# Twelve unread small products and a re-planned first part in a decayed linear attention with two feed-forward layers

## The chip, the cores and the metric

One core of a Trainium2 chip runs the whole program. The metric is device time in microseconds from one launch; lower is better. Several executions are timed, and one of them is profiled.

## The reference

A recurrent attention over 4 batches, 8 heads, 768 steps and 48 features, then two feed-forward layers over the 3072 tokens of width 384:

```python
for t in range(S):
    cur = einsum('bhd,bhe->bhde', u[None] * kt, vt)
    y[:, :, t] = einsum('bhd,bhde->bhe', rt, state + cur)
    state = wt[:, :, :, None] * state + einsum('bhd,bhe->bhde', kt, vt)
...
h = maximum(maximum(x @ w1, x @ w2), x @ w3)          # 384 -> 768
x = h @ w_out                                         # 768 -> 384
silu = g * (1.0 / (1.0 + exp(-g)))                    # g = x @ w_gate, 384 -> 1536
out = silu * (x @ w_val) @ w_out
```

## The kernel before

**Attention.** The 768 steps are six chunks of 128 (c = 0 to 5), and a chunk has four units (a pair of heads each, in the order 3, 0, 1, 2), so 24 units n = 0 to 23. Unit 4 is the first of chunk 1. For each unit SyncE loads the decays, k and r (`load_a`, tile inpA, two DMAs, two buffers), and v (`load_v`). VectorE then runs two scans over the decays (`suffix` L366, `prefix` L379), makes the scaled k and r (`khats` L369 and L371, tile kh; `rps` L382, tile rp), and for units 0 to 7 the product rk (L426), which TensorE sums (`rk_sum` L432, tile pa) and ScalarE spreads over a diagonal (`diag` L447, tile A). TensorE transposes kh (`transposes` L469, tile kp), ScalarE copies it out (`keep`), TensorE makes the state's increment (`outer` L536, tile kv) and the scores (`scores` L455, tile sc), which VectorE writes into A under a mask (`causal` L460). The output y is built in two parts (`first_y`, and `second_y` with L495 and L508). Between them ScalarE reads two columns (`peek`). The second part needs the state decayed to the middle of the chunk: `add_state` (L549), `decay` (L393). ScalarE copies y out rounded (`upper` L557), TensorE subtracts that copy (`take_upper` L566), and the rest is kept too (`lower`).

**Feed-forward.** Every wide product is three TensorE products of 128x512 (high times high, high times low, low times high; `mm3`, L590 to L592). A piece `up(c, f, m)` is nine of them, with weight group f. The weights arrive as 64-bit floats (`wload`, two buffers). VectorE turns them to 32 bits in three steps (`bits`, L131 to L133), ScalarE rounds the high part (`whigh` L629), VectorE subtracts for the low part (`wlow` L634, tile lo). Chunk 0's pieces wait for these. `up_out` takes the maximum over m = 0, 1, 2 on VectorE (L664). `down` makes the first layer's output, with plain 32-bit products in chunk 0 (L681). Behind chunk 5's first layer only the second layer runs.

**The order.** Nothing of this is scheduled by hand. Each step is added to a `Plan` with its engine, a cost in us, its dependencies, a due time, and the accumulator buffers (`slot`) it takes of a pool of four (`psM`). `Plan.order` simulates the engines with these costs and emits the steps in the order of their simulated starts; each engine then executes its own in that order. Among steps that can start about as early it takes the one with the lowest due time plus 15 times the start; `STAY` takes 2.0 off for a step of the same `kind` as the engine's last. The attention's products on TensorE have kind 1, all else kind 0. Every unit has a due time of its own (`due`).

**Guards.** ScalarE checks the decays' range (`watch`, two passes over 128x512), in place for units 8 to 23, and for units 0 to 7 from a second load late in the program (`watch_load`).

Of the kernel before, what the change touches and what calls it, by code (L numbers as in the profile page):

```python
# [9 lines left out]
F32 = mybir.dt.float32  # L10
# [4 lines left out]
AF = mybir.ActivationFunctionType  # L15
# [7 lines left out]
NT = 512  # L23
D = 48
G = 4
# [12 lines left out]
class Plan:  # L38
# [4 lines left out]
    SLOTS = 4  # L43
    STAY = 2.0

    def __init__(self):
        self.items = []

    def add(self, eng, cost, fn, deps=(), due=None, lat=0.1, slot=0, after=0.0, slack=0.0, kind=0):
        t = dict(kind=kind, eng=eng, cost=cost, fn=fn, deps=[d for d in deps if d is not None], due=due, lat=lat,  # L50
                 slot=slot, after=after, slack=slack, readers=[], id=len(self.items), start=None, end=None)
        self.items.append(t)
        return t
# [6 lines left out]
    def order(self):  # L60
# [18 lines left out]
        for t in reversed(topo):  # L79
            dates = [n["due"] - n["cost"] - t["lat"] for n in t["next"]] + [t["due"] or far]  # L80
            t["due"] = min(dates)
        free, last, dma, slots, out = {}, {}, 0.0, [], []
        for t in items:
            t["todo"] = len(t["deps"])
        avail = [t for t in items if not t["todo"]]
        while avail:
# [14 lines left out]
            for t in avail:  # L101
                if t.get("at") is not None and t["at"] <= best + 0.3:
                    k = first.get(t["eng"])
                    t["key"] = t["due"] + 15 * t["at"] - self.STAY * (t["kind"] == last.get(t["eng"]))
                    if k is None or t["key"] < k["key"]:
                        first[t["eng"]] = t
# [3 lines left out]
            avail.remove(t)  # L110
            last[t["eng"]] = t["kind"]
            t["start"] = t["at0"]
# [162 lines left out]
def fused(ctx: ExitStack, tc: tile.TileContext, pk, ub, wt_all, out):  # L275
# [264 lines left out]
    def add_state(n, s):  # L540
        c, j = units[n]
        if c == 0 and s == 0:
            decay(n, 0)
            for g in range(G):
                nc.scalar.activation(
                    states[n][1][:, g, :], kvs[n][0][:, g, :], AF.Copy, scale=total[n % 2][:, 2 * g + 1:2 * g + 2]
                )
        else:
            nc.vector.tensor_tensor(states[n][1] if s == 0 else S[j], states[n][s], kvs[n][s], ALU.add)  # L549
# [98 lines left out]

    hh, hl, hws, pss = {}, {}, {}, {}

    def up(c, f, m):
# [123 lines left out]
    def on(eng, cost, fn, *args):  # L775
        return lambda deps=(), due=None, **k: p.add(eng, cost, lambda: fn(*args), deps, due, **k)
# [19 lines left out]

    chunks = list(range(8)) + [("again", i) for i in range(8)] + list(range(8, 20)) + [("late", n) for n in range(8)]
    for turn, what in enumerate(chunks):
# [53 lines left out]
    for n, (c, j) in enumerate(units):  # L852
# [3 lines left out]
        cold = 1.4 if early else 1.0  # L856
        due = 10 + 6.0 * i if early else START[c - 1] + (i + 1) * (PERIOD / 4) - (30 if c == 5 else 6 if c == 1 else 18)
        war = prev("rp", n, 2) + prev("kh", n, 2) + prev("prefix", n, 2)
# [20 lines left out]
        if c > 0:  # L879
            de = L["decay0", n] = on("DVE", 0.27, decay, n, 0)([to] + prev("state1", n, 4) + prev("y2", n, 2))  # L880
        if n >= 8:
            for k in range(2):
                L[f"watch{k}", n] = on("ACT", 0.81, watch, n, k)([la, r_])
        tr = L["tr", n] = on("PE", 0.45 * cold, transposes, n)([kh] + prev("outer", n, 1), slot=1, slack=lag, kind=1)
        kT = L["khT", n] = p.reads(on("ACT", 0.48, keep, n)([tr] + prev("outer", n, 1)), tr)
        o = L["outer", n] = on("PE", 0.55 * cold, outer, n)([kT, lv], slot=2 - c // 5, slack=lag, kind=1)
        st = L["state0", n] = on("ACT" if early else "DVE", 0.9 if early else 0.25, add_state, n, 0)([o, de or to] + (prev("y2", n, 2) if early else []))
        p.reads(st, o)
        d1 = L["decay1", n] = st if early else on("DVE", 0.27, decay, n, 1)([st, to])
        if c < NC_ - 1:  # L890
            L["state1", n] = p.reads(on("DVE", 0.25, add_state, n, 1)([o, d1], due + 2), o)
        sc_ = L["scores", n] = on("PE", 0.6 * cold, scores, n)([r_] + prev("causal", n, 1), slack=lag, kind=1)
        ca = L["causal", n] = on("DVE", 0.66, causal, n)([sc_, L["diag1", n]])
        before_y = prev("lower", n, 1)
        if n in LENT:
            before_y = [on("PE", 0.8, lend, n)(before_y + L["x", n - 3], slack=lag, kind=1)]
        y1_ = L["y1", n] = on("PE", 0.3 * cold, first_y, n)([ca, lv] + before_y, slack=lag, kind=1)
        pe = on("ACT", 0.15, peek, n)([y1_])
        y = L["y2", n] = on("PE", 0.9 * cold, second_y, n)([pe, d1], slack=lag, kind=1)

# [19 lines left out]
        if i == 3:  # L920
# [23 lines left out]
            for m, k in sorted(turns, key=lambda t: t[1]) if c == 5 else turns:  # L944
# [12 lines left out]
                L["hw", 9 * c + 6 + m] = [w2]  # L957
            L["chain"] = before


# [19 lines left out]
    for c in range(NC_):  # L980
# [58 lines left out]
        if c == 2:  # L1039
            checks = [t for k in range(8) for t in L["late", k]] + [t for i in range(8) for t in L["again", i]]  # L1040
            checks += [t for i in range(8, 20) for t in L["check", i]]
            rows = on("DVE", 0.8, check_rows)(checks, base + 30)
            mt = on("PE", 0.3, check_mat)([rows], base + 34, slot=1)
            p.reads(on("DVE", 0.2, check_end)([mt], base + 38), mt)
# [81 lines left out]
```

## Time and profile before

| | us |
|---|---|
| median of 3 runs | 865.78 |
| lowest, highest | 860.95, 868.53 |
| profiled execution, whole | 860.6 |
| its span, first to last instruction | 858.8 |
| TensorE busy in the span | 838.9 |
| VectorE busy | 426.8 |
| ScalarE busy | 342.4 |

The profile names TensorE PE, its weight loads PEld, VectorE DVE, ScalarE ACT, GpSimd POOL and SyncE SP. L590 is line 590 of the kernel. PEclk is the granted TensorE clock: 1.00 is 2.4 GHz and 0.50 is 1.2 GHz. Ends of products are modelled, so the time from one start to the next says what a product costs.

### The profile page before, as it was taken

How to read it: one execution, taken by the hardware profiler on the slowest of the kernel's cores; microseconds unless marked ns; L12 is line 12 of the kernel's file. 1: busy time of each engine (PE TensorE's matmuls, PEld its weight loads, DVE VectorE, ACT ScalarE, POOL GpSimd, SP SyncE). 2: the span in 40 equal slices, each digit the busy share in tenths (PEclk: the TensorE clock that was granted, in tenths of full speed). 3: DMA queues.
4: the chain of work that ended last, by engine and by line, in shares of the span. 5: the costliest groups of instructions: out<-in, count | busy, mean ns of one | idle time of the engine just before them, and what ended most of it. 6: DMA issues, size and time to landing. Idle time of an engine off the chain costs nothing.

```text
span 858.8 us, 15114 instructions
## 1 busy us (share of the span) xinstructions
PE 838.9 (98%) x6352; PEld 679.2 (79%) x6352; DVE 426.8 (50%) x612; ACT 342.4 (40%) x738; POOL 78.4 (9%) x104
## 2 busy tenths in 40 slices
PE   6799999999999999999999999999999999999997
PEld 5678578878788788788888888888888888888885
DVE  7899997466565666389783222222222121212121
ACT  6544565454555554454557321221232122212121
POOL 1001351211112000012000100100010010000000
PEclk9899999999999999999999999999999999999999
DMA  8766584544536542244533200010020000000001
GB/s 235 199 187 219 135 224 101 157 134 119 156 74 158 146 162 72 81 182 166 192 122 93 71 3 1 25 49 1 1 74 0 1 13 38 0 1 37 1 0 41
DMA packets 24379, 78.82 MB, mean 92 GB/s; under 512 B 3888, under 2 KB 7088, under 8 KB 20720
## 3 DMA queue, kind: packets, MB, share of 16 engines
q1 hardware_dynamic: 24304, 77.78, 30.5%
q8 instruction: 52, 0.85, 0.4%
q14 instruction: 23, 0.19, 0.1%
HBM read 66.23 MB, written 9.44 MB: 88 GB/s over the span
## 4 chain that ended last, share of the span: by engine, by line
PE 94%; DVE 2%; ACT 1%; DMA 1%; issue 1%; SPq 0%; DVEq 0%; ACTq 0%
PE ps L590 12%; PE ps L591 11%; PE ps L592 11%; PE po L590 6%; PE pv L591 6%; PE pg L591 6%; PE po L591 6%; PE pg L590 6%; PE pv L590 6%; PE po L592 6%; PE pg L592 6%; PE pv L592 6%; PE y L495 2%; PE kv L536 1%; PE sc L455 1%; PE ps L681 1%
## 5 line engine op out<-in xcount | busy, mean ns | idle before, releaser
L738 DVE TENSOR_TENSOR sil<-sil,pv 128x512 f32<-128x512 f32 x72 | 49.5, 687 | 246.3 <-PE pv L592 240.1
L590 PE MATMUL ps<-xh,hi 128*128 128x512 f32 x324 | 130.3, 402 | 0.0
L592 PE MATMUL ps<-xh,lo 128*128 128x512 f32 x324 | 126.5, 390 | 0.0
L591 PE MATMUL ps<-xl,hi 128*128 128x512 f32 x324 | 126.4, 390 | 0.0
L735 ACT ACTIVATE sil<-pg 128x512 f32<-128x512 f32 x72 | 42.9, 596 | 155.8 <-PE pg L592 155.8
L742 ACT ACTIVATE ph<-sil 128x512 fp32r<-128x512 f32 x72 | 45.4, 630 | 124.8 <-DVE sil L738 124.8
L591 PE MATMUL pg<-yl,hi 128*128 128x512 f32 x216 | 84.5, 391 | 0.0
L591 PE MATMUL pv<-yl,hi 128*128 128x512 f32 x216 | 84.5, 391 | 0.0
L591 PE MATMUL po<-pl,hi 128*128 128x512 f32 x216 | 84.5, 391 | 0.0
L590 PE MATMUL po<-ph,hi 128*128 128x512 f32 x216 | 84.4, 391 | 0.0
L590 PE MATMUL pg<-yh,hi 128*128 128x512 f32 x216 | 84.3, 390 | 0.0
L590 PE MATMUL pv<-yh,hi 128*128 128x512 f32 x216 | 84.3, 390 | 0.0
L592 PE MATMUL pg<-yh,lo 128*128 128x512 f32 x216 | 84.0, 389 | 0.0
L592 PE MATMUL po<-ph,lo 128*128 128x512 f32 x216 | 84.0, 389 | 0.0
L592 PE MATMUL pv<-yh,lo 128*128 128x512 f32 x216 | 84.0, 389 | 0.0
L747 DVE TENSOR_TENSOR pl<-sil,ph 128x512 fp32r<-128x512 f32 x72 | 49.8, 692 | 58.4 <-ACT ph L742 58.4
L590 PEld LDWEIGHTS ps<-xh,hi 128*128 128x128 f32 x324 | 60.8, 188 | 13.8
L592 PEld LDWEIGHTS ps<-xh,lo 128*128 128x128 f32 x324 | 60.8, 188 | 13.0
L591 PEld LDWEIGHTS ps<-xl,hi 128*128 128x128 f32 x324 | 60.9, 188 | 11.5
L664 DVE TENSOR_TENSOR hw<-hw,ps 128x512 f32<-128x512 f32 x60 | 40.9, 682 | 35.6 <-PE ps L592 34.0
L723 POOL TENSOR_TENSOR yl<-y,yh 128x512 fp32r<-128x512 f32 x18 | 24.2, 1348 | 353.4 <-ACT yh L719 353.3
L447 ACT ACTIVATE A<-stacked,a 128x64 f32<-128x64 f32 x192 | 49.4, 337 | 2.6 <-DVE a L419 2.4
(126 smaller groups left out, 1333.1 us busy)
## 6 DMA issues: line engine op xcount, KB each, us to landing
raw<-wt SPq DMA_DIRECT2D x28, 1152.0 KB, 5.3
inpA<-pk SPq DMA_DIRECT2D x44, 294.0 KB, 5.2
inpT<-pk SPq DMA_DIRECT2D x16, 384.0 KB, 4.6
inpV<-pk SPq DMA_DIRECT2D x24, 200.0 KB, 3.5
y1d<-y1s SPq DMA_DIRECT2D x18, 256.0 KB, 2.3
y<-y1d SPq DMA_DIRECT2D x18, 256.0 KB, 2.7
outT<-os SPq DMA_DIRECT2D x18, 256.0 KB, 2.0
wl<-pk SPq DMA_DIRECT2D x8, 272.0 KB, 2.7
```

The source lines that it names most:

```text
L447: nc.scalar.activation(A[n][:, i, :], stacked, AF.Copy, scale=sums[n][:, k:k + 1])
L455: nc.tensor.matmul(sc[n][t, a, T * g:T * g + T], khat[n][q, g, t], rp[n % 2][q, g, t], start=True, stop=True)
L495: nc.tensor.matmul(ys[n][64 * h:64 * h + rows, a, C * b + T * s:C * b + T * s + T], inpV[n][t, D * i:D * i + rows], A[n][t, i, :], start=( ...
L590: nc.tensor.matmul(ps, lh, rh, start=first, stop=False)
L591: nc.tensor.matmul(ps, lh, rl, start=False, stop=False)
L592: nc.tensor.matmul(ps, ll, rh, start=False, stop=last)
L664: nc.vector.tensor_tensor(hws[f], hws[f], pss[c, f, m], ALU.max)
L723: nc.gpsimd.tensor_tensor(yl[c, m], y1[m], yh[c, m].bitcast(F32), ALU.subtract)
L735: nc.scalar.activation(sil[f % 3], pgs[f % 3, 0], AF.Silu)
L738: nc.vector.tensor_tensor(sil[f % 3], sil[f % 3], pgs[f % 3, 1], ALU.mult)
L742: nc.scalar.activation(h_, sil[f % 3], AF.Copy)
L747: nc.vector.tensor_tensor(l_, sil[f % 3], prod[c, f][0].bitcast(F32), ALU.subtract)
```

## The change

`stir` makes eight products of the 128x128 tile `minus` with itself into an accumulator that nobody reads. Twelve of them are added to the plan at a cost of 0.6, not to start before 9, 10, ... 20 us of the plan, with due times from 36 us on. The `kind` and `STAY` rule goes. In chunk 0 the state's first half is copied by one ScalarE instruction and decayed by VectorE, in place of four scaled ScalarE copies. Units 4 to 7 are watched in place, so only four late loads remain. The due times of chunk 1's units come 12 us earlier.

```diff
-    STAY = 2.0
...
-                    t["key"] = t["due"] + 15 * t["at"] - self.STAY * (t["kind"] == last.get(t["eng"]))
-                    if k is None or t["key"] < k["key"]:
+                    if k is None or t["due"] + 15 * t["at"] < k["due"] + 15 * k["at"]:
...
-            for g in range(G):
-                nc.scalar.activation(
-                    states[n][1][:, g, :], kvs[n][0][:, g, :], AF.Copy, scale=total[n % 2][:, 2 * g + 1:2 * g + 2]
-                )
+            nc.scalar.activation(states[n][1], kvs[n][0], AF.Copy)
...
+    def stir():
+
+        ps = psM.tile([128, NT], F32, tag="mm", name="stir")
+        for k in range(8):
+            nc.tensor.matmul(ps[:, 0:128], minus, minus, start=True, stop=True)
...
-    chunks = list(range(8)) + [("again", i) for i in range(8)] + list(range(8, 20)) + [("late", n) for n in range(8)]
+    chunks = list(range(8)) + [("again", i) for i in range(8)] + list(range(8, 20)) + [("late", n) for n in range(4)]
...
-        due = 10 + 6.0 * i if early else START[c - 1] + (i + 1) * (PERIOD / 4) - (30 if c == 5 else 6 if c == 1 else 18)
+        due = 10 + 6.0 * i if early else START[c - 1] + (i + 1) * (PERIOD / 4) - (30 if c == 5 else 18)
...
-        if n >= 8:
+        if not early:
             for k in range(2):
                 L[f"watch{k}", n] = on("ACT", 0.81, watch, n, k)([la, r_])
...
-        st = L["state0", n] = on("ACT" if early else "DVE", 0.9 if early else 0.25, add_state, n, 0)([o, de or to] + (prev("y2", n, 2) if early else []))
+        st = L["state0", n] = on("ACT" if early else "DVE", 0.25, add_state, n, 0)([o, de] + (prev("y2", n, 2) if early else []))
...
-        d1 = L["decay1", n] = st if early else on("DVE", 0.27, decay, n, 1)([st, to])
+        d1 = L["decay1", n] = on("DVE", 0.27, decay, n, 1)([st, to])
...
+    for k in range(12):
+        on("PE", 0.6, stir)([], START[0] + 4 + k, slot=1, after=9.0 + 1.0 * k)
```

Three places show what the planner makes of it. The changed program's lines are 3 lower up to `add_state` (L363 is the scan of L366) and 6 lower from there to the new function (L584 to L586 are L590 to L592, L628 is L634).

VectorE, before, from unit 3's rp on: two bit steps of weight group 0 (raw), unit 3's mask and state, the first bit step of group 1, unit 4's first scan, and group 0's low half (lo).

```order
L382 TENSOR_TENSOR rp_103<-inpA_94,F 128x512
L132 SCALAR_TENSOR_TENSOR raw<-raw,tmp 128x1152
L133 SCALAR_TENSOR_TENSOR raw<-raw 128x1152
L460 COPY_PREDICATED A<-mask,sc 128x512
L549 TENSOR_TENSOR S_106<-s_576,kv 128x192
L131 TENSOR_SCALAR tmp<-raw 128x1152
L366 SCALAR_TENSOR_TENSOR I<-inpA_93,d1r 128x520
L634 TENSOR_TENSOR lo<-raw,hi 128x1152
```

VectorE, changed, from the first bit step of group 0 to its third.

```order
L128 TENSOR_SCALAR tmp<-raw 128x1152
L363 SCALAR_TENSOR_TENSOR I<-inpA_93,d1r 128x520
L423 TENSOR_TENSOR rk<-inpA_93 128x512
L457 COPY_PREDICATED A<-mask,sc 128x512
L366 RECIPROCAL d1f<-I 128x8
L368 TENSOR_TENSOR kh<-inpA_93,I 128x512
L390 TENSOR_TENSOR s_609<-s_609,total_100 128x192
L376 SCALAR_TENSOR_TENSOR F<-inpA_93,d1f 128x520
L129 SCALAR_TENSOR_TENSOR raw<-raw,tmp 128x1152
L379 TENSOR_TENSOR rp_102<-inpA_93,F 128x512
L390 TENSOR_TENSOR s_674<-S_107,total_99 128x192
L130 SCALAR_TENSOR_TENSOR raw<-raw 128x1152
```

Unit 4's scan, rk, kh and rp now stand ahead of group 0's second and third bit steps; before, the scan came behind them. Behind the last row come unit 4's mask, unit 3's state, group 1's first bit step, unit 4's state and decay, and then group 0's low half.

TensorE, before, where the feed-forward begins: the end of unit 3, then the first piece.

```order
L508 MATMUL y<-rp_103,s_576 48x64 x8
L566 MATMUL y<-xh,minus 128x256 x2
L590 MATMUL ps<-xh,hi 128x512
L591 MATMUL ps<-xl,hi 128x512
L592 MATMUL ps<-xh,lo 128x512
```

TensorE, changed, at the same place: the end of unit 3, unit 4's output and state increment with two stirs, then the first piece.

```order
L560 MATMUL y<-xh,minus 128x256 x2
L492 MATMUL y<-A,inpV 64x64 x8
L533 MATMUL kv<-inpV,khT 64x48 x16
L649 MATMUL stir<-minus 128x128 x8
L492 MATMUL y<-A,inpV 64x64 x8
L505 MATMUL y<-rp_102,s_674 48x64 x8
L505 MATMUL y<-rp_102,s_675 48x64 x8
L649 MATMUL stir<-minus 128x128 x8
L560 MATMUL y<-xsh,minus 128x256 x2
L584 MATMUL ps<-xh,hi 128x512
```

Unit 4's pa, transposes and scores stand ahead of these rows, among unit 3's. Before, all of unit 4 was spread between the pieces.

TensorE, before, around unit 5's output, among the pieces of weight group 3.

```order
L592 MATMUL ps<-xh,lo 128x512
L495 MATMUL y<-A,inpV 64x64 x8
L508 MATMUL y<-rp_103,s_893 48x64 x8
L508 MATMUL y<-rp_103,s_894 48x64 x8
L590 MATMUL ps<-xh,hi 128x512
```

TensorE, changed, around unit 5's output, among the pieces of weight group 1.

```order
L492 MATMUL y<-A,inpV 64x64 x8
L649 MATMUL stir<-minus 128x128 x8
L492 MATMUL y<-A,inpV 64x64 x8
L505 MATMUL y<-rp_103,s_939 48x64 x8
L505 MATMUL y<-rp_103,s_940 48x64 x8
L649 MATMUL stir<-minus 128x128 x8
L584 MATMUL ps<-xh,hi 128x512
```

Two of the seven stirs behind the first piece stand here; two stand around unit 5's scores and increment, and three in a row (24 products) behind the next piece, ahead of weight group 2. Of the other five, one is behind unit 0's transposes, one behind its scores, one ahead of unit 3's increment, and two are in the rows further up.

## Rows read from the trace of the kernel before

**Rows 1.** The page, part 4: shares of the chain that ended last.

```profile
PE 94%; DVE 2%; ACT 1%; DMA 1%; issue 1%; SPq 0%; DVEq 0%; ACTq 0%
```

**Rows 2.** Stretches: length, busy per engine (instructions), clock, DMA share, GB/s.

```profile
core 0: us, PE busy (x) PEld busy (x) DVE busy (x) ACT busy (x) POOL busy (x), PEclk, DMA share, GB/s
...
25.60:30.84 5.24, 5.20 (x92) 4.73 (x92) 5.21 (x7) 2.91 (x12) 0.00 (x0) 0.50 0.89 172
30.84:36.50 5.66, 3.43 (x100) 2.62 (x93) 4.50 (x7) 3.72 (x9) 1.17 (x1) 1.00 0.62 118
36.50:72.90 36.40, 36.34 (x403) 29.07 (x402) 34.92 (x46) 15.07 (x34) 1.16 (x1) 1.00 0.63 191
72.90:111.40 38.50, 37.28 (x484) 24.73 (x482) 38.18 (x54) 21.87 (x61) 12.20 (x13) 1.00 0.67 178
111.40:450.00 338.60, 338.24 (x3198) 272.73 (x3195) 230.38 (x326) 174.24 (x377) 45.05 (x59) 1.00 0.46 139
450.00:852.80 402.80, 402.80 (x1770) 331.53 (x1768) 94.50 (x143) 109.07 (x194) 15.54 (x12) 1.00 0.07 23
```

**Rows 3.** TensorE's timeline: start, us, line, names, shape, count, idle before.

```profile
25.64 1.87 PE L432 MATMUL pa<-inpA,rk 128*128 128x2 f32 x8 [2.99 <-DVE rk L426]
...
36.17 0.51 PE L566 MATMUL y<-xh,minus 128*128 128x256 f32 x2 [0.72 <-ACT xh L557]
36.52 0.40 PE L590 MATMUL ps<-xh,hi 128*128 128x512 f32 x1
...
38.59 0.95 PE L432 MATMUL pa<-inpA,rk 128*128 128x2 f32 x8
39.41 0.48 PE L590 MATMUL ps<-xh,hi 128*128 128x512 f32 x1
...
43.59 0.60 PE L469 MATMUL kp<-ident,kh 128*128 128x128 f32 x4
44.12 0.69 PE L455 MATMUL sc<-rp,kh 64*64 64x64 f32 x32
...
50.41 0.46 PE L495 MATMUL y<-A,inpV 64*64 64x64 f32 x16
...
51.25 0.50 PE L590 MATMUL ps<-xh,hi 128*128 128x512 f32 x1
...
72.93 0.40 PE L590 MATMUL ps<-xh,hi 128*128 128x512 f32 x1
```

**Rows 4.** Unit 4's loads on SyncE's queue, issued 21.1 and 21.4.

```profile
L350 SPq DMA_DIRECT2D inpA<-pk x2: 311/366/422, 21.1 to 21.4; - x2
...
DMA to landing us min/median/max: 7.4/8.2/9.0
```

**Rows 5.** VectorE's timeline: start, us, line, names, shapes, count.

```profile
28.18 1.35 DVE L132 SCALAR_TENSOR_TENSOR raw<-raw,tmp 128x1152 int32<-128x1152 int32 x1
...
36.16 1.35 DVE L132 SCALAR_TENSOR_TENSOR raw<-raw,tmp 128x1152 int32<-128x1152 int32 x1
37.43 0.68 DVE L426 TENSOR_TENSOR rk<-inpA 128x512 f32<-128x512 f32 x1
38.04 0.19 DVE L369 RECIPROCAL d1f<-I 128x8 f32<-128x8 f32 x1
...
38.71 1.35 DVE L133 SCALAR_TENSOR_TENSOR raw<-raw 128x1152 int32<-128x1152 int32 x1
39.99 1.23 DVE L379 TENSOR_TENSOR_SCAN F<-inpA,d1f 128x520 f32<-128x520 f32 x1
41.14 0.33 DVE L393 TENSOR_TENSOR s<-S,total 128x192 f32<-128x192 f32 x1
41.39 0.68 DVE L382 TENSOR_TENSOR rp<-inpA,F 128x512 f32<-128x512 f32 x1
41.99 1.35 DVE L634 TENSOR_TENSOR lo<-raw,hi 128x1152 fp32r<-128x1152 f32 x1
43.86 0.75 DVE L131 TENSOR_SCALAR tmp<-raw 128x1152 int32<-128x1152 int32 x1
```

**Rows 6.** The page, part 5: a ScalarE pass over 128x512; busy, mean ns, idle before.

```profile
L735 ACT ACTIVATE sil<-pg 128x512 f32<-128x512 f32 x72 | 42.9, 596 | 155.8 <-PE pg L592 155.8
```

More of the change, by code (lines that the diff above doesn't have):

```diff
@@ L43, with add @@
     SLOTS = 4
-    STAY = 2.0
     def __init__(self):
         self.items = []
-    def add(self, eng, cost, fn, deps=(), due=None, lat=0.1, slot=0, after=0.0, slack=0.0, kind=0):
-        t = dict(kind=kind, eng=eng, cost=cost, fn=fn, deps=[d for d in deps if d is not None], due=due, lat=lat,
+    def add(self, eng, cost, fn, deps=(), due=None, lat=0.1, slot=0, after=0.0, slack=0.0):
+        t = dict(eng=eng, cost=cost, fn=fn, deps=[d for d in deps if d is not None], due=due, lat=lat,
                  slot=slot, after=after, slack=slack, readers=[], id=len(self.items), start=None, end=None)
@@ L81, in order @@
             t["due"] = min(dates)
-        free, last, dma, slots, out = {}, {}, 0.0, [], []
+        free, dma, slots, out = {}, 0.0, [], []
         for t in items:
@@ L110, in order @@
             avail.remove(t)
-            last[t["eng"]] = t["kind"]
             t["start"] = t["at0"]
@@ L880, in fused @@
             de = L["decay0", n] = on("DVE", 0.27, decay, n, 0)([to] + prev("state1", n, 4) + prev("y2", n, 2))
-        if n >= 8:
+        if not early:
             for k in range(2):
                 L[f"watch{k}", n] = on("ACT", 0.81, watch, n, k)([la, r_])
-        tr = L["tr", n] = on("PE", 0.45 * cold, transposes, n)([kh] + prev("outer", n, 1), slot=1, slack=lag, kind=1)
+        tr = L["tr", n] = on("PE", 0.45 * cold, transposes, n)([kh] + prev("outer", n, 1), slot=1, slack=lag)
         kT = L["khT", n] = p.reads(on("ACT", 0.48, keep, n)([tr] + prev("outer", n, 1)), tr)
-        o = L["outer", n] = on("PE", 0.55 * cold, outer, n)([kT, lv], slot=2 - c // 5, slack=lag, kind=1)
-        st = L["state0", n] = on("ACT" if early else "DVE", 0.9 if early else 0.25, add_state, n, 0)([o, de or to] + (prev("y2", n, 2) if early else []))
+        o = L["outer", n] = on("PE", 0.55 * cold, outer, n)([kT, lv], slot=2 - c // 5, slack=lag)
+        st = L["state0", n] = on("ACT" if early else "DVE", 0.25, add_state, n, 0)([o, de] + (prev("y2", n, 2) if early else []))
         p.reads(st, o)
-        d1 = L["decay1", n] = st if early else on("DVE", 0.27, decay, n, 1)([st, to])
+        d1 = L["decay1", n] = on("DVE", 0.27, decay, n, 1)([st, to])
         if c < NC_ - 1:
             L["state1", n] = p.reads(on("DVE", 0.25, add_state, n, 1)([o, d1], due + 2), o)
-        sc_ = L["scores", n] = on("PE", 0.6 * cold, scores, n)([r_] + prev("causal", n, 1), slack=lag, kind=1)
+        sc_ = L["scores", n] = on("PE", 0.6 * cold, scores, n)([r_] + prev("causal", n, 1), slack=lag)
         ca = L["causal", n] = on("DVE", 0.66, causal, n)([sc_, L["diag1", n]])
@@ L895, in fused @@
         if n in LENT:
-            before_y = [on("PE", 0.8, lend, n)(before_y + L["x", n - 3], slack=lag, kind=1)]
-        y1_ = L["y1", n] = on("PE", 0.3 * cold, first_y, n)([ca, lv] + before_y, slack=lag, kind=1)
+            before_y = [on("PE", 0.8, lend, n)(before_y + L["x", n - 3], slack=lag)]
+        y1_ = L["y1", n] = on("PE", 0.3 * cold, first_y, n)([ca, lv] + before_y, slack=lag)
         pe = on("ACT", 0.15, peek, n)([y1_])
-        y = L["y2", n] = on("PE", 0.9 * cold, second_y, n)([pe, d1], slack=lag, kind=1)
+        y = L["y2", n] = on("PE", 0.9 * cold, second_y, n)([pe, d1], slack=lag)
         room = [L["up", c - 2, 5, 2]] if c >= 2 else []
@@ L1039, in fused @@
         if c == 2:
-            checks = [t for k in range(8) for t in L["late", k]] + [t for i in range(8) for t in L["again", i]]
+            checks = [t for k in range(4) for t in L["late", k]] + [t for i in range(8) for t in L["again", i]]
             checks += [t for i in range(8, 20) for t in L["check", i]]
```

## The prediction

> **What bounds the kernel now.** I read the chain of waits first: 94% of the span lies on TensorE's own work [rows 1]. An average over stages says little, so the stretches come next [rows 2]. From 450 us to 852.8 TensorE is busy for 402.80 of 402.80 us, and from 111.4 to 450 for 338.24 of 338.60. Nothing off TensorE can move those stretches; they start when the work before them is done. So the change is decided before 111.4 us, by three things: when the first feed-forward piece starts (36.52 us [rows 3]), how much work TensorE then has up to 111.4, and how long it stands still: 0.06 us in 36.5 to 72.9 and 1.22 us in 72.9 to 111.4 [rows 2]. VectorE is just as full in that last stretch (38.18 of 38.50 us) and is the engine that could take over.
>
> **The change part by part.** The order of the changed program shows two moves that matter. Unit 4 (the first of chunk 1) is now done wholly before the first feed-forward piece, where before the first piece came right behind unit 3. And of the twelve stirs, five stand before the first piece, seven between the first pieces: around unit 5, the last three in a row ahead of group 2.
>
> *When the first piece starts.* VectorE now reaches unit 4's scan before it has finished the first weight group. Before, it had done everything of units 0 to 3 but unit 3's mask, with the first bit step of group 0, at 28.18 us [rows 5]. Now three decays (0.25 us each, as 41.14 to 41.39 in rows 5) and little else come on top, so it is at the scan by some 29 us. Unit 4's loads were issued at 21.1 and 21.4 us and took 7.4 and 9.0 us to land [rows 4], so the second is there at 30.4. Nobody minded before, since the scan came later; now VectorE stands still for it. I keep 30.4, since the load waits for the same product of unit 2 on VectorE as before; 28.5 (the first load's landing) is the lower bound, 32 the upper (unit 2 one stir's cold length, 1.6 us, later).
>
> From the scan to the end of group 0's low half VectorE has these, start to start from rows 5: two scans 2 x 1.15, rk 0.61, reciprocal and kh 0.67, rp 0.60, two bit steps 1.27 + 1.28, the first bit step of group 1 0.75, three decays 0.75, two state sums of the decays' size 0.50, the low half 1.27 (it is as long as a bit step, 1.35), and two masked copies, taken as rk (same elements) 1.22. Sum 11.22, so 41.6 us. The last decay ends one low half earlier, 40.4. On it waits the second part of unit 4's output, 0.84 (50.41 to 51.25 [rows 3]), then a stir of 0.82, which covers the wait for ScalarE's copy (0.72 at 36.17), then the subtraction, 0.35 (36.17 to 36.52). The first piece starts at 40.4 + 2.01 = 42.4 us, 5.9 later than before.
>
> In that time unit 4 is done. Its price: from 36.52 to 72.93 TensorE did 13 pieces, unit 4 and unit 5, without a pause. A piece is 36.52 to 38.59 = 2.07, so 13 are 26.9, and a unit is (36.41 - 26.9) / 2 = 4.75. Lateness here: 5.9 - 4.75 = **+1.15 us**.
>
> *A stir.* No row of before shows one. It is eight products of 128 columns with a 128x128 weight load each. From below: columns alone, a quarter of a 512-column product (2.07 / 9 = 0.23), 8 x 0.0575 = 0.46. From above: the four transposes (also 128 columns, own weights) take 43.59 to 44.12 = 0.53, so 8 are 1.06. Between them: the eight instructions of pa load 128x128 each and stream two columns, and take 38.59 to 39.41 = 0.82. I take 0.82, since that row has the weight loads and next to no columns. The planner's own number in the source is 0.6.
>
> The Trainium skill ("TensorE: Matmul & The Clock Gate", Back-to-back issue gap) gives some 81 ns for a load and product pair at 128 columns, against 103 ns a load in rows 3. By it a stir would be 0.65, the seven 4.5, and the sum 4.5 instead of 5.7.
>
> The five early stirs fall into standstill. The two behind unit 0's transposes and scores push TensorE by up to 2 x 1.64 if they run at the clock's lower level (pa takes 1.87 there, 0.95 at the other); but TensorE stood 2.99 us at 25.64 for unit 3's rk, which hangs on a load and VectorE [rows 3], and eats it up there. The other three lie between unit 3's transposes and the first piece, where VectorE's 11.2 us set the pace; the one on the path is counted.
>
> The seven behind the start lie on a TensorE that has no pause: 7 x 0.82 = **+5.74 us**, bounds 3.2 and 7.4. Would VectorE have made it wait there anyway? Group 2's low half is VectorE's twenty-second piece behind group 0's: four bit steps 5.1, two first bit steps 1.4, two scans 2.3, two more low halves 2.5, kh, rk, rp and mask 2.5, three maxima 1.8 (as rk), five small ones 1.25; 16.9 in all, so 58.5 us. TensorE without stirs gets there at 42.4 + 6 x 2.07 + 4.75 = 59.6, with them at 65.3. It waits in neither case, and VectorE is 7 us ahead afterwards.
>
> *What comes back.* That lead removes the 1.22 us of standing still in 72.9 to 111.4: **-1.2 us**. From there on it is the same work in the same density.
>
> *The other edits.* Without the planner's bonus for staying with one kind, eleven visits of transposes and scores are split by a piece. The first product of a piece behind small ones is 0.08 longer (0.48 at 39.41, 0.40 at 36.52), so up to +0.9; small products of unlike shapes also wait for each other, so as much may come back. I take 0. Chunk 0's state as one copy and a VectorE decay: the decays are in the sums above. Eight watches of chunk 1 move to ScalarE's early part, 0.6 us each (a pass over 128x512 [rows 6]) where it is busy 15.07 of 36.40 us; their four loads and passes leave a stretch where TensorE never waited. Both 0. The lead of VectorE and ScalarE covers them; without it, one watch ahead of a copy that TensorE needs would cost 0.6.
>
> **Sum:** 1.15 + 5.74 - 1.2 = +5.7 us. The profiled execution took 860.6 us with a span of 858.8, so 866.3 on its scale. The median of the runs shown is 865.78, 5.2 above it and near the upper one, so 871.5 on the median's scale, +0.7%. About 1% is what a measurement of this kernel can tell from no change.
>
> **The rivals.** *The stirs are hidden.* If VectorE, with its new decays and late scan, reaches group 2's low half only after 65.3 us, the seven fall into waits that are there anyway: the sum is 1.15 - 1.2, no change, 865.8. For it: the stirs were planned where TensorE stands still, and VectorE is full. Against it: 58.5 leaves 7 us. It decides from 59.6 on, and fully only at 65.3.
>
> *The clock stays up: not slower.* Between 25.6 and 30.84 the granted clock was 0.50, the 1.2 GHz level, behind the 2.99 us standstill, with TensorE busy 5.20 of 5.24 us [rows 2, 3]. If the early stirs shorten that standstill enough, the stretch runs at 2.4 GHz and 2.6 us come back, if they are on the path at all (I have VectorE's load there). If the runs at the median hold 5.2 us more of such stretches and lose these too, the result is 871.5 - 2.6 - 5.2 = 863.7. For it: the runs spread by 7.6 us, and something varies. Against it: no row shows that it is the clock. The Trainium skill (same page, What's actually happening) has it that the throttled clock is the default and activity releases it; by that the stirs buy clock, as the low stretch behind a standstill agrees.
>
> *The clock falls at the start.* While TensorE waits for unit 4 (for rk, rp, the mask and the decay in turn) it stands still more than before, and the clock can fall to 1.2 GHz as it did around 24 us. That stretch lasted 6.8 us; one such over the first pieces costs at most half, 3.4: 874.9. For it: unit 4's 4.75 us are spread over some 12. Against it: the stirs, and the stretch 30.84 to 36.5 kept 1.00 with 3.43 busy of 5.66 us.
>
> **How the numbers follow.** Forecast 50%: the known bounds put it between 867 (stir 0.46, loads at 28.5) and 875 (stir 1.06, loads at 32, splits at their worst). Clock falls 20%, stirs hidden 15%, clock stays up 15%. The range 864 to 879 takes in the lower two rivals and the clock's fall on top of a dear stir. Over 1% slower means above 874.4: half of the clock's fall, the top of the forecast's own range and what I have missed, 28%. Over 1% faster needs more than the whole of the best rival, 6%. The rest, 66%, is within 1%.
>
> **What would show it.** Right: in the changed profile VectorE waits for the load inpA ahead of unit 4's scan, near 29 to 30 us; the first feed-forward product starts near 42.4; a stir takes 0.7 to 0.9 us start to start at full clock; the three in a row before group 2 follow each other with no idle time before the next piece but their own; TensorE stands still under 0.5 us from 73 us on, and the first piece of chunk 1 starts some 6 us later than 111.4. Wrong: a wait of TensorE on a low half in groups 1 or 2 (stirs hidden), a first piece before 40 us, a granted clock of 0.50 behind 36 us, or stirs of under 0.5 us.

## The result, and the profile after

| | before | after |
|---|---|---|
| median, us | 865.00 (6 runs) | 874.06 (6 runs) |
| lowest, highest | 860.95, 868.53 | 871.29, 877.28 |
| ratio after to before, 95% interval | | 1.0095 [1.0074, 1.0117] |
| profiled execution, its span | 860.6, 858.8 | 871.29, 869.5 |

The changed kernel is 0.95% slower by the ratio, some 8.2 us (the two medians shown differ by 9.1, which is inside the interval); the forecast was +5.7 us (0.66%). The range and the case "within 1%" held, but 0.66% lies below the interval. About 2.5 us are missing from the sum. The profiled executions differ by 10.7 us: that of before lies 4.4 us under its median, that of after 2.8.

The page of after, part 4, the chain that ended last:

```profile
PE 90%; DVE 3%; ACT 3%; DMA 1%; issue 1%; SPq 0%; ACTq 0%; DVEq 0%
```

TensorE still sets the end. The stretches of after, with the columns of [rows 2]:

```profile
core 0: us, PE busy (x) PEld busy (x) DVE busy (x) ACT busy (x) POOL busy (x), PEclk, DMA share, GB/s
28.55:31.96 3.41, 3.41 (x70) 2.80 (x71) 3.38 (x6) 3.16 (x11) 0.11 (x1) 0.50 0.71 159
31.96:43.81 11.85, 10.08 (x254) 8.95 (x255) 11.11 (x18) 7.91 (x22) 0.46 (x1) 1.00 0.47 106
...
43.81:80.50 36.69, 36.69 (x392) 31.14 (x391) 33.97 (x44) 17.71 (x41) 5.03 (x5) 1.00 0.66 197
80.50:117.90 37.40, 37.40 (x330) 24.36 (x330) 34.32 (x45) 20.13 (x53) 13.60 (x15) 1.00 0.61 173
117.90:459.00 341.10, 338.90 (x3266) 270.67 (x3265) 227.47 (x326) 173.45 (x375) 39.49 (x54) 1.00 0.47 137
459.00:863.00 404.00, 404.00 (x1777) 332.79 (x1775) 95.34 (x144) 104.17 (x180) 15.54 (x12) 1.00 0.06 20
```

From the first feed-forward piece to 117.9 us TensorE does not pause at all, where before it stood still for 0.06 and 1.22 us [rows 2]. The last stretch is the same work at the same pace. New is the stretch 117.9 to 459: 2.2 us of standing still, against 0.36 between 111.4 and 450 before. The prediction had "under 0.5 us from 73 us on" among its signs of being right; that holds up to 117.9 us and not behind it.

TensorE's timeline of after (start, us, line, names, shape, count, idle before), the places that the prediction spoke of:

```profile
10.88 1.10 PE L452 MATMUL sc<-rp,kh 64*64 64x64 f32 x32
11.91 1.97 PE L649 MATMUL stir<-minus 128*128 128x128 f32 x8
13.67 1.81 PE L429 MATMUL pa<-inpA,rk 128*128 128x2 f32 x8
15.41 0.71 PE L492 MATMUL y<-A,inpV 64*64 64x64 f32 x16
...
19.53 1.13 PE L452 MATMUL sc<-rp,kh 64*64 64x64 f32 x32
...
39.85 0.46 PE L492 MATMUL y<-A,inpV 64*64 64x64 f32 x16 [0.75 <-ACT xl L569]
40.10 0.66 PE L533 MATMUL kv<-inpV,khT 64*64 64x48 f32 x32
40.69 1.11 PE L649 MATMUL stir<-minus 128*128 128x128 f32 x8
41.73 0.46 PE L492 MATMUL y<-A,inpV 64*64 64x64 f32 x16
42.02 0.63 PE L505 MATMUL y<-rp,s 64*48 64x64 f32 x32
42.57 1.11 PE L649 MATMUL stir<-minus 128*128 128x128 f32 x8
43.52 0.46 PE L560 MATMUL y<-xsh,minus 128*128 128x256 f32 x2
43.81 0.40 PE L584 MATMUL ps<-xh,hi 128*128 128x512 f32 x1
...
53.41 1.00 PE L649 MATMUL stir<-minus 128*128 128x128 f32 x8
54.34 0.69 PE L452 MATMUL sc<-rp,kh 64*64 64x64 f32 x32
...
64.16 2.79 PE L649 MATMUL stir<-minus 128*128 128x128 f32 x24
66.78 0.44 PE L584 MATMUL ps<-xh,hi 128*128 128x512 f32 x1
...
428.12 0.50 PE L584 MATMUL pg<-yh,hi 128*128 128x512 f32 x1 [0.89 <-ACT sil L735]
```

- The first piece starts at 43.81 us, 7.29 later than at 36.52 [rows 3]. Less unit 4's 4.75 that is 2.5 us, against 1.15 forecast.
- TensorE runs from 39.85 to 43.81 without a pause, and both stirs of that stretch stand in it. The first takes 40.69 to 41.73, 1.04 us.
- The first stir behind a piece takes 53.41 to 54.34, 0.93 us. Three in a row take 64.16 to 66.78, 0.87 each. All seven behind the first piece take 6.5 us, start to start.
- At 11.91 a stir takes 1.76 us. The pa behind it takes 13.67 to 15.41, 1.74, against 0.82 in [rows 3]. These are the lengths of the lower level, 1.2 GHz, though the profile shows no low clock so early.

Three rows of before at the same place, which show what the early stirs push:

```profile
10.32 1.10 PE L455 MATMUL sc<-rp,kh 64*64 64x64 f32 x32
11.35 1.87 PE L432 MATMUL pa<-inpA,rk 128*128 128x2 f32 x8
...
16.57 0.94 PE L455 MATMUL sc<-rp,kh 64*64 64x64 f32 x32
```

The second scores start at 16.57 before and at 19.53 now. VectorE waits for them, as its timeline of after shows:

```profile
20.80 0.73 DVE L457 COPY_PREDICATED A<-mask,sc 128x512 f32<-128x512 uint8 x1 [2.64 <-PE sc L452]
...
29.88 0.75 DVE L128 TENSOR_SCALAR tmp<-raw 128x1152 int32<-128x1152 int32 x1
30.55 1.23 DVE L363 TENSOR_TENSOR_SCAN I<-inpA,d1r 128x520 f32<-128x520 f32 x1
...
41.19 0.36 DVE L390 TENSOR_TENSOR s<-s,total 128x192 f32<-128x192 f32 x1
41.47 1.35 DVE L628 TENSOR_TENSOR lo<-raw,hi 128x1152 fp32r<-128x1152 f32 x1
```

Unit 4's scan starts at 30.55, almost where I had it (30.4), but no wait for its load stands before it. VectorE is simply late, because it waited 2.64 us for scores that stood behind stirs. Two kernels further down leave the early stirs out (none issued, and the last seven alone) and show that these are the cause: VectorE waits 0.94 and 0.93 us for the same scores, stands still for unit 4's load (0.73 and 0.60 us), as I had it, and starts the scan at 28.90 and 28.98.

The new wait at 427 us is ScalarE's. Its timeline of after:

```profile
420.20 1.23 ACT L623 ACTIVATE hi<-raw 128x1152 fp32r<-128x1152 f32 x1 [4.33 <-DVE raw L130]
...
426.17 1.28 ACT L735 ACT_TABLE_LOAD   x1
427.47 0.60 ACT L735 ACTIVATE sil<-pg 128x512 f32<-128x512 f32 x1
```

And of before:

```profile
409.57 1.24 ACT L629 ACTIVATE hi<-raw 128x1152 fp32r<-128x1152 f32 x1 [3.37 <-DVE raw L133]
...
416.86 0.60 ACT L735 ACTIVATE sil<-pg 128x512 f32<-128x512 f32 x1
```

The first gate piece starts at 409.48 before and at 418.82 after, 9.3 later. ScalarE's rounding of a weight group and its first `sil` come 10.6 later, so ScalarE has lost another 1.3 us against TensorE, and the buffer that `sil` must empty is late by 0.89. The chain behind it begins with the weight words on VectorE (raw L130).

### The profile page after: what moved, and what is told of

It reads as the page before. It is cut to its first block, busy times and chain, and to the rows that moved or that the text cites. A ratio compares the mean times of both kernels' runs of the same rounds, so it can differ in the third digit from the quotient of the medians.

```text
span 869.5 us, 15307 instructions
## 1 busy us (share of the span) xinstructions
PE 851.6 (98%) x6448; PEld 689.7 (79%) x6448; DVE 426.4 (49%) x616; ACT 340.7 (39%) x726; POOL 77.9 (9%) x104
## 4 chain that ended last, share of the span: by engine, by line
PE 90%; DVE 3%; ACT 3%; DMA 1%; issue 1%; SPq 0%; ACTq 0%; DVEq 0%
PE ps L584 10%; PE ps L585 9%; PE ps L586 9%; PE po L584 6%; PE po L585 6%; PE po L586 6%; PE pg L584 6%; PE pg L585 6%; PE pv L585 6%; PE pv L584 6%; PE pg L586 5%; PE pv L586 5%; PE y L492 2%; PE sc L452 2%; PE stir L649 1%; PE kv L533 1%
## 5 line engine op out<-in xcount | busy, mean ns | idle before, releaser
L584 PE MATMUL ps<-xh,hi 128*128 128x512 f32 x324 | 131.5, 406 | 0.0
L586 PE MATMUL ps<-xh,lo 128*128 128x512 f32 x324 | 126.6, 391 | 0.0
L584 PE MATMUL pg<-yh,hi 128*128 128x512 f32 x216 | 84.5, 391 | 0.9 <-ACT sil L735 0.9
L584 PE MATMUL po<-ph,hi 128*128 128x512 f32 x216 | 84.5, 391 | 0.0
L584 PE MATMUL pv<-yh,hi 128*128 128x512 f32 x216 | 84.4, 391 | 0.0
L586 PE MATMUL po<-ph,lo 128*128 128x512 f32 x216 | 84.0, 389 | 0.0
L586 PE MATMUL pg<-yh,lo 128*128 128x512 f32 x216 | 84.0, 389 | 0.0
L586 PE MATMUL pv<-yh,lo 128*128 128x512 f32 x216 | 84.0, 389 | 0.0
L584 PEld LDWEIGHTS ps<-xh,hi 128*128 128x128 f32 x324 | 60.8, 188 | 13.6
L586 PEld LDWEIGHTS ps<-xh,lo 128*128 128x128 f32 x324 | 60.8, 188 | 13.2
```

Source lines behind the costliest of these rows:

```text
L584: nc.tensor.matmul(ps, lh, rh, start=first, stop=False)
L586: nc.tensor.matmul(ps, ll, rh, start=False, stop=last)
```

## The experiments

Theory A is the prediction's: the stirs behind the first piece are work on a TensorE that has no pause, and everything else in the change costs nothing. Theory B: the stirs fall into standstill, and another edit costs the time. Theory C: the stirs change the clock. All ratios are to the kernel before, run on the same chip in the same rounds; a difference of two of them is uncertain by 2 to 3 us, and by 3 to 5 where a kernel has six runs.

**The stirs planned but not issued** (changed kernel):

```diff
-    def stir():
+    def stir(n):
+        if n not in ():
+            return
```

> The changed kernel with the twelve stirs planned but not issued, so every other step keeps its place. Own price (the stirs are TensorE time that nothing hides): the seven behind the first feed-forward piece took 6.5 us in the changed profile and the five early ones push that piece by some 2, so 865.5 (864 to 867), level with before; first piece near 41.5 us. Re-plan (the new order costs it, the stirs are hidden): 872 or more. Clock (the stirs keep TensorE at 2.4 GHz and pay for part of themselves): 869 or more, with a longer stretch at 1.2 GHz ahead of the first piece.

Measured 1.0034 [1.0010, 1.0058], median 870.31. That is above what A gave, and by the time it is C's number, "869 or more, with a longer stretch at 1.2 GHz ahead of the first piece". Its clock, in the columns as above:

```profile
32.38:46.03 13.65, 12.07 (x194) 9.73 (x194) 12.48 (x16) 7.70 (x21) 0.34 (x1) 0.50 0.48 129
```

The low stretch lasts 13.65 us against 3.41 in the changed kernel, and the first piece (42.24 here) stands in it. In the runs it can be seen too: the four with a mean granted clock of 0.994 or more took 866.5 to 866.9 us, the eight with 0.991 or less 869.3 to 872.1. So this kernel is not the changed one less its stirs at an equal clock, and 1.0034 holds some of the clock's price.

TensorE's timeline of this kernel, its waits between 57 and 80 us:

```profile
58.73 0.46 PE L492 MATMUL y<-A,inpV 64*64 64x64 f32 x16 [1.17 <-ACT seen L518]
...
66.78 1.02 PE L429 MATMUL pa<-inpA,rk 128*128 128x2 f32 x8 [0.54 <-PE ps L586]
...
73.23 0.69 PE L452 MATMUL sc<-rp,kh 64*64 64x64 f32 x32 [0.69 <-DVE rp L379]
...
77.85 0.46 PE L492 MATMUL y<-A,inpV 64*64 64x64 f32 x16 [1.21 <-DVE A L457]
```

With the stirs taken out TensorE does wait here, 3.6 us in four places, and 1.35 more at 118.6. None of the four is the wait that I looked at (group 2's low half): they stand ahead of the attention's own steps (`y`, pa, sc), three of them behind ScalarE or VectorE. So the planner's gaps are partly real, and the stirs there need not be paid in full.

**No stirs in the plan at all:**

```diff
-    for k in range(12):
-        on("PE", 0.6, stir)([], START[0] + 4 + k, slot=1, after=9.0 + 1.0 * k)
```

> The changed kernel without the twelve stirs in the plan, so that the planner orders the rest anew, still without the bonus for one kind. Own price: 865 (863 to 868), like the kernel with planned but unissued stirs, since the order hardly matters where TensorE has no pause. Re-plan: the order is what costs, so it differs from the kernel with planned but unissued stirs by 3 us or more.

Measured 1.0021 [1.0000, 1.0043], median 867.84. The changed kernel's 1.0095 less this is 0.0074: **the stirs cost 6.4 us** (0.0074 x 865; each ratio is uncertain by 0.2%, so some 4 to 9). The other 0.2% is left for the other edits. The time is inside A's range (863 to 868); planned and unissued stirs differ from none by 0.0013, which is not clear of noise.

**The first five stirs alone, and the last seven alone** (in the function of the first run, the numbers that are issued):

```diff
-        if n not in ():
+        if n not in (0, 1, 2, 3, 4):
```

> The changed kernel with only the five stirs ahead of the first feed-forward piece issued, the other seven planned but not issued. Own price: 6.5 us under the changed kernel, 867.5 (866 to 869). Re-plan: as the changed kernel, 873 to 875. Clock: below the kernel with no stir issued, since these five stand where TensorE would stand still and cost nothing else.

> The changed kernel with only the seven stirs behind the first feed-forward piece issued, the first five planned but not issued. Own price: 872 (870.5 to 873.5), 6.5 us over the kernel with none issued. Re-plan: as the changed kernel and as the one with none issued, 872 or more each, no difference between them. Clock: above the changed kernel, since the early five are missing.

Measured 1.0044 [1.0018, 1.0069] for the five and 1.0071 [1.0046, 1.0096] for the seven, each inside A's range. Against the plan without issued stirs (1.0034) the five add 0.9 us, which is inside the uncertainty, and the seven 3.2. Next to the five the seven add 1.0095 - 1.0044, 4.4 us. So the seven cost 3 to 4.5 us where their own length is 6.5, each number uncertain by 2 to 3. The traces agree where the clock doesn't differ: from the first piece to the first piece of chunk 1 TensorE takes 69.92 us with the five alone (42.65 to 112.57) and 73.38 in the changed kernel (43.81 to 117.19), both at 1.00, so the seven add 3.5 there. With the five alone it stands still for 2.3 us of that stretch, in the changed kernel not at all.

The five are not free either: with them the first piece starts at 42.65, without them (the seven alone) at 40.90. But eight of the twelve runs with the five alone have a mean clock of 0.996 or more, and none of the twelve with no stir issued. That is C in part: the five give back through the clock some of what they cost, and no gain is left.

With the seven TensorE has one pause left of over 0.02 us between its first piece and 240 us:

```profile
40.90 0.39 PE L584 MATMUL ps<-xh,hi 128*128 128x512 f32 x1
...
45.38 1.02 PE L429 MATMUL pa<-inpA,rk 128*128 128x2 f32 x8 [0.21 <-PE ps L586]
```

**The last seven with sixteen products each:**

```diff
-        for k in range(8):
+        for k in range(8 if n < 5 else 16):
```

> The changed kernel with sixteen products in each of the last seven stirs instead of eight. Own price: the first dose took 6.5 us of TensorE and cost some 3.2 to 4.4, the rest standing where TensorE would have waited; in the changed profile no such wait is left between 44 and 117 us, so the second dose is paid in full, 6.5 us on top of the changed kernel, a ratio of 1.017 (1.0145 to 1.019) to the kernel before. Hidden stirs: waits are left to fill, so 1.0095 to 1.012.

Measured 1.0204 [1.0156, 1.0251], median 883.4, above the expected range: 0.0109 above the changed kernel, 9.4 us (uncertain by 4.5) for 6.5 us of added products. No pause is left to take the second dose. But the run isn't clean, as its stretches show (columns as above):

```profile
29.30:39.50 10.20, 8.46 (x219) 7.38 (x215) 9.88 (x16) 7.90 (x28) 0.57 (x1) 1.00 0.65 132
39.50:53.10 13.60, 12.91 (x148) 11.18 (x140) 9.23 (x12) 4.64 (x11) 0.50 (x1) 0.50 0.50 152
```

The clock fell to 0.50 at 39.5, ahead of the first piece (48.52 here), and stayed there for 13.6 us, although TensorE was busy for 12.91 of them. How much of the 9.4 is the clock's can't be told from this run.

**The planner's bonus back, no stirs** (the lines of `kind` and `STAY` as before, the loop of stirs taken out):

```diff
+                    t["key"] = t["due"] + 15 * t["at"] - self.STAY * (t["kind"] == last.get(t["eng"]))
-                    if k is None or t["due"] + 15 * t["at"] < k["due"] + 15 * k["at"]:
+                    if k is None or t["key"] < k["key"]:
```

> The changed kernel without stirs in the plan, with the bonus for one kind (STAY) put back. If losing the bonus costs (unit 23 ends later, so the second layer's first weights come later and TensorE waits 0.8 us for silu near 425 us, as in all four variants so far): 1 to 2 us under the variant without the bonus, 866.5, ratio 1.000 to 1.001, and no such wait. If the bonus is worth nothing: ratio 1.0021 as there, and the wait stays.

Measured 0.9995 [0.9975, 1.0014], median 864.85, all twelve runs between 863.72 and 865.70. Without the bonus it was 1.0021, so the bonus is worth about 0.26%, 2.2 us, as expected; the two were run on different chips and the difference is hardly clear of noise, and the next kernel gives a second reading on the same chip. ScalarE in this kernel, where the changed one has its new wait:

```profile
412.97 1.23 ACT L626 ACTIVATE hi<-raw 128x1152 fp32r<-128x1152 f32 x1 [2.73 <-DVE raw L133]
...
420.23 0.60 ACT L738 ACTIVATE sil<-pg 128x512 f32<-128x512 f32 x1
```

The first gate piece starts at 413.52 here, so `sil` follows after 6.71 us; in the changed kernel it is 427.47 - 418.82 = 8.65, before 416.86 - 409.48 = 7.38. TensorE waits for `sil` only in the changed one. The kernel without stirs and without bonus waits there too, for 0.81 us. All seven profiled kernels without the bonus have this wait (0.75 to 0.94 us), none of the six with it, stirs or not.

The rest of the bonus's worth stands ahead of it. From the first piece of chunk 1 to the first gate piece the kernel without bonus takes 301.99 us (114.27 to 416.26), this one 300.64 (112.88 to 413.52), both at 1.00: 1.35 us more, of which 0.93 is standstill (1.80 against 0.87). With the 0.81 that is 2.2 us.

**Chunk 1's due times back, no stirs, no bonus:**

```diff
-        due = 10 + 6.0 * i if early else START[c - 1] + (i + 1) * (PERIOD / 4) - (30 if c == 5 else 18)
+        due = 10 + 6.0 * i if early else START[c - 1] + (i + 1) * (PERIOD / 4) - (30 if c == 5 else 6 if c == 1 else 18)
```

> The changed kernel without stirs in the plan, with the due times of chunk 1 put back 12 us later, so that the first feed-forward piece stands ahead of unit 4 again. If the later start costs (first piece at 41.8 us instead of 36.5, with 4.75 us of unit 4 done in return): first piece near 37 us, ratio 1.000, 1 to 2 us under the variant without it. If TensorE's work is what counts: as that variant, 1.002.

Measured 1.0017 [0.9996, 1.0038], median 866.67, the case in which TensorE's work is what counts. The first piece starts at 35.66 us, 6.2 earlier than in the same kernel with the new due times (41.84), and the time is the same. So unit 4's place, which moves the first piece by 6 us, is worth nothing that can be measured. The wait for `sil` stays (0.92 us, up to 422.2): it isn't the due times that bring it. On the same chip this kernel is 1.8 us above the one with the bonus (866.67 against 864.85), and ten of its twelve runs lie above all twelve of that one. The two differ in the due times as well; if those are worth nothing, the bonus is worth some 2 us, seen twice, and the wait for `sil` is 0.8 to 0.9 of it.

**The kernel before with the twelve stirs in its plan:**

```diff
+    for k in range(12):
+        on("PE", 0.6, stir)([], START[0] + 4 + k, slot=1, after=9.0 + 1.0 * k)
```

> The kernel before with the twelve stirs added to its plan and nothing else; seven come ahead of the first feed-forward piece and five behind it. Own price: the five behind the start cost 0.93 each, 4.6, on a TensorE that had 0.06 us of pause there, and the seven ahead push the first piece by 1 to 3; 6 to 7.5 together, ratio 1.007 to 1.009. Clock: the stirs take the stretch at 1.2 GHz away and give 2.6 back, ratio 1.004 or less. Re-plan: the stirs cost nothing, ratio 1.000 to 1.002.

Measured 1.0103 [1.0065, 1.0141], median 874.15: 8.9 us (5.6 to 12.2) for twelve stirs and nothing else, somewhat over the expected 6 to 7.5. One stretch of its profiled execution:

```profile
28.58:49.06 20.48, 19.85 (x222) 18.48 (x223) 14.97 (x19) 9.08 (x26) 0.50 (x1) 0.50 0.65 151
```

TensorE is busy for 19.85 of 20.48 us there and is granted 0.50 throughout; in the kernel before, the low stretch was over at 30.84 [rows 2]. The clock rises at 49.06, with the first feed-forward piece (46.80) under way. This execution is one of two of the six with a mean clock under 0.99 (878.5 and 879.6 us); the other four, at 0.994 to 0.996, took 872.3 to 875.2. So the stirs cost in either case, and the low clock adds some 5.

**The changed kernel with the bonus back** (the edit of the kernel without stirs above, the stirs kept):

> The changed kernel with the bonus for one kind put back, twelve stirs planned and issued, seven ahead of the first feed-forward piece and five behind it. Own price, and the two causes add: the changed kernel's 1.0095 less the 0.0026 that the bonus gave back without stirs, 1.007 (1.0045 to 1.009). Bonus alone: if losing it were the whole loss, 1.000 to 1.002. Clock: if the spread of the stirs decided, no better than 1.0095.

Measured 1.0155 [1.0122, 1.0189], median 879.17: the expectation was missed, and on the wrong side. TensorE's timeline:

```profile
12.28 1.97 PE L652 MATMUL stir<-minus 128*128 128x128 f32 x8
...
39.08 1.80 PE L652 MATMUL stir<-minus 128*128 128x128 f32 x8
40.68 0.52 PE L481 MATMUL y<-xsh,shift 128*128 128x256 f32 x1
...
52.45 1.97 PE L652 MATMUL stir<-minus 128*128 128x128 f32 x8
54.22 0.73 PE L587 MATMUL ps<-xh,hi 128*128 128x512 f32 x1
54.75 0.63 PE L588 MATMUL ps<-xl,hi 128*128 128x512 f32 x1
...
57.31 0.51 PE L588 MATMUL ps<-xl,hi 128*128 128x512 f32 x1
57.65 0.40 PE L589 MATMUL ps<-xh,lo 128*128 128x512 f32 x1
```

Here the whole first part runs at the lower level, by the lengths of its products: a stir takes 1.60 us at 39.08 and 1.77 at 52.45, a wide product 0.43 to 0.53 until 57.3 and 0.23 behind it. The plan puts seven of the twelve stirs ahead of the first piece. They take 1.60 to 1.88 each, start to start, 12.4 us together, and the first piece starts 12.6 later than without stirs (54.22 against 41.60). The other five at 0.93 add 4.7. That sum, 17.1, is close to the difference of the two profiled spans, 880.9 - 862.9 = 18.0. In this execution nearly nothing of the stirs is hidden, though the low clock also lengthens the other products, and the sum doesn't tell the two apart. The profiled execution was the slowest of its six; the medians differ by 14.3.

So the edits do not add. Without stirs the bonus saves 2.2 us; with them the kernel with the bonus is 0.006, some 5 us, slower than the changed one, since the planner then puts seven stirs and not five ahead of the first piece.

**The kernel before with the state step and the early watches alone** (bonus and due times as before, no stirs):

> The kernel before with its bonus and its due times, no stirs, and only the changed state step (one ScalarE copy and a VectorE decay) and the watches of units 4 to 7 in place. If these two edits are hidden: 1.000 (0.998 to 1.002). If the five decays of 0.25 us on a full VectorE and the eight watches of 0.6 us cost: 1.002 to 1.005. It is also the candidate for a version faster than both, at 0.997, if the shorter state step on ScalarE frees the first part.

Measured 1.0010 [0.9987, 1.0033], median 866.35. These two edits do nothing that can be measured.

**Stirs in the pauses that TensorE really has.** The kernel with the bonus and without planned stirs, with six stirs of five products put by hand behind steps where its trace shows TensorE standing still:

```diff
+        fill = [L["tr", 0], L["tk", 1], L["scores", 4], L["y2", 5], L["tr", 6], L["y2", 6]]
...
             t["fn"]()
+            if any(t is f for f in fill):
+                stir()
```

> The version with the bonus and without planned stirs, with six stirs of five products each put by hand at six places where its profile shows TensorE standing still for 0.69 to 1.30 us (behind unit 0's transposes, unit 1's subtraction, unit 4's scores, unit 5's output, unit 6's transposes and unit 6's output). Own price: at 0.12 us a product they fit, 0.6 each, so they cost nothing: 0.9995 (0.998 to 1.001). Clock: if activity there pays, 0.998 or less and a higher mean clock. If a stir costs wherever it stands: 6 x 0.6 = 3.6 us, 1.0035 or more.

Measured 1.0016 [0.9998, 1.0034], against 0.9995 without them: just above the range for stirs that fit, and well under the price of stirs that cost wherever they stand. TensorE's standstill from its first product to 800 us falls from 7.85 to 5.91 us, and the last low stretch of the clock ends as early (32.95 against 33.20, the latter by the lengths of products), yet nothing is gained. Even well placed, these stirs are at best free.

## Why the prediction was right, and where its sum was short

**The direction was right for the reason given.** The stirs are the cost: 6.4 of some 8.2 us, by the kernel without them; the kernel before with them added loses 8.9. "Stirs hidden" and "the clock stays up" are out as forecasts of the time, though there is a part in each: the seven do fill 2.3 us of pauses, and the clock does respond to the early stirs. "The clock falls at the start" (874.9) is nearer to the measured median than my 871.5, and it isn't refuted: the profiled execution has 1.00 from 31.96 us on, but it is the fastest of the six, and two of the others have a lower mean clock (0.991 against 0.996 and 0.997; 874.17 and 877.28 us).

**What comes back, -1.2:** right up to 117.9 us: TensorE has no pause from 43.8 on, and chunk 1's first piece starts 5.8 us later (117.19 against 111.39), where I had said some 6. That this agrees so well is luck. The first piece alone was 1.4 us later than forecast and the seven 0.75 dearer. What makes up for it is mostly work put off: in the changed kernel TensorE has done the scores of 9 units and 8 state increments when that piece starts, and before 10 and 9, with half a unit's first output besides. Before, these products stand last ahead of that piece, from 109.46 to 111.39 with a wait of 0.38, so some 1.5 us come behind 117.19 now. From there on the two profiled executions part by another 4.9 us: these 1.5, 1.8 more of standstill, and some 1.5 that I can't place. So most of what is missing from the sum lies behind the stretch that I added up.

**The first piece:** 43.81 where I said 42.4, by a mechanism that wasn't the one I named. "VectorE now stands still for it" (unit 4's load) didn't occur. The early stirs, at twice their length under the lower clock, hold back scores for which VectorE waits 2.64 us, and unit 4's scan comes at 30.55 for that reason and at 28.9 without them; that it fell near my 30.4 is luck. The step that failed is that TensorE's later standstill eats the early stirs up: with the seven alone the first piece starts at 40.90, 2.9 us earlier than with all twelve. A second miss is that one stir was counted on the path to the first piece where two stand in TensorE's last run without a pause.

**A stir, 0.82:** mis-sized; 0.87 to 0.95 at full clock (1.04 ahead of `y`) and 1.60 to 1.88 at the lower level, inside the bounds of 0.46 and 1.06 for full clock. The row of pa (weight loads with two columns) was a good neighbour; a stir is about a tenth longer. The figure of the Trainium skill ("TensorE: Matmul & The Clock Gate", Back-to-back issue gap), by which I worked out 0.65, was further off: these products take 109 to 119 ns each at full clock, not 81.

**"It waits in neither case":** wrong as a whole, though right for the low half that I checked. Without the stirs TensorE waits some 3.6 us between 57 and 80 and 1.35 at 118.6, ahead of the attention's steps. So the seven cost 3.2 to 4.4 us net (3.5 in the traces) and not 5.74. Checking one late piece of VectorE doesn't show that there is no other.

**The other edits, 0:** right for unit 4's place, the state step and the watches, and wrong for the bonus. I let up to 0.9 us of split visits cancel against as much; without stirs the runs put the loss of the bonus at about 2, of which 0.8 to 0.9 is the new wait for `sil`, far from the place of the change.

**The sum as the runs have it:** stirs 6.4, bonus 2.2, the rest -0.4 (0.9995), together 8.2; each is a difference of two ratios and uncertain by 2 to 3 us. It holds for this order alone, stirs taken out first and the bonus put back then; put back first, the bonus makes the time longer by some 5 us, and the stirs then cost 13.8. Against my terms the seven were 1.5 to 2.5 too dear; the early stirs (put at nothing but the one in the 1.15) and the bonus were too cheap.

What stays open: how the 6.4 divide between the products themselves and the longer time at the lower clock. The runs of one kernel differ by up to 11 us (877.11 to 888.32 with the double stirs), and for most kernels I could tie that to the clock only in part. For the kernel before it is the clock in the main, which the prediction said no row shows: of the 81 runs of it beside the experiments 63 have a mean granted clock under 0.997, and among these the time falls as the clock rises, from 868.0 to 869.6 us at 0.985 and 0.986 (4 runs) over 862.5 to 865.6 at 0.991 (13) to 860.7 to 863.4 at 0.996 (5). The 18 with higher readings lie anywhere from 862.9 to 869.9; the kernel with bonus and stirs shows that such a reading (0.998) can hide a low first part. Stirs with more columns weren't tried. No version beat the kernel before: the one with the bonus and without stirs equals it.

## What to carry to other kernels

A planner's standstill is not the chip's: before work is put into it, look in the trace at what TensorE waits for there, since filler ahead of a product for which another engine waits delays that engine too. On an engine that sets the end, expect filler to cost its full length as soon as the real pauses are used up, and nearly double under the lower clock (a stir took 0.87 to 1.04 us, and 1.60 to 1.88). When a change is a bundle, take its edits back one by one and in more than one order: here the one that looked like housekeeping (the loss of the bonus) seems to cost a quarter of the whole once the stirs are out and to save time while they are in, and the one that moved the first piece by 6 us (unit 4's place) costs nothing that can be measured. Compare runs at a like clock where the record has it.

## What the runs showed of the hardware

- A TensorE that is busy can stay at the lower level. It was busy for 19.85 of 20.48 us at 0.50 in the kernel before with stirs, and by the lengths of its products it ran the whole first part at the lower level, up to 57.3 us, in the one with bonus and stirs. In both the clock rose with the first feed-forward pieces under way. The Trainium skill ("TensorE: Matmul & The Clock Gate", What's actually happening) says that activity releases the throttle; in these two stretches TensorE was at work and the throttle stayed.
- The clock isn't the same in nearly equal programs, nor in all runs of one: the five early stirs of the changed kernel are unchanged in the one with double later stirs, and yet that one fell to 0.50 at 39.5 us where the changed one had 1.00 from 31.96 on, and the runs of the kernel before read 0.985 to 0.999 in the mean.
- A PEclk of 1.00 at the very start of a span isn't to be trusted: the page of after shows full clock in its first slices, while a pa took 1.74 us there and the same products 0.82 later (47.92 to 48.74).
